# Three x blocks' second forms made during gate/up and kept in DRAM, loads asked earlier, some splits and streamed loads moved

## The chip, the cores and the metric

One core of one Trainium2 chip runs the whole kernel in one launch. The metric is the device time in microseconds, the median of three runs. The engines are named as in the profile: PE is TensorE (matmuls), DVE is VectorE, ACT is ScalarE, POOL is GpSimd (here it only issues DMAs), SP is SyncE (it issues DMAs).

## What is computed

```python
# x: [1, 2048, 512]; g = sigmoid of one dot product per row
g = sigmoid((x * gate_w).sum(-1, keepdims=True))
a = x @ dft_hid_re.T ; b = x @ dft_hid_im.T           # 512 x 512 each
fnet = dft_seq_re @ a - dft_seq_im @ b                # 2048 x 2048 each
h = silu(x @ w1) * (x @ w3)                           # 512 -> 1376
mlp = h @ w2                                          # 1376 -> 512
out = g * fnet + (1 - g) * mlp
```

All in fp32. The kernel splits each fp32 operand into a high part (rounded to fp32r, the type that the matmul takes) and a low part (the rest), and multiplies high x high, high x low and low x high, so each product costs three matmuls.

## The kernel before

**Block products.** Each product of 2 x 2 blocks takes seven block products in place of eight (a Strassen-like scheme with the sums T1 to T4 on one side and similar sums on the other). An operand therefore exists in forms: raw blocks and sums or differences of them, each split into a high part (`high`: a copy on ACT into fp32r) and a low part (`low`: a subtraction on DVE). A product of one 128-row weight half against a 512-wide operand is three matmuls (`mm3`, line 122), and a gate/up product is two such halves: six matmuls.

**Gate/up.** The hidden size is cut into 11 chunks and x into two halves g; `ITEMS` lists 22 pairs (chunk, half): chunks 0 to 8 with half 0, chunks 9 and 10 with both, then chunks 0 to 8 with half 1. Item 0 is written out by hand; `gate_up(n)` does items 1 to 21. Each full item issues seven products on PE: X += (wb form 4), Z = (wb form 5), `first1(n+3)`, X += (wb form 3), Z += (wa form 2), `first2(n+3)`, X += (wb form 6). The last three items have five. The bank X of item n is n modulo 4. Between the products, in program order, stand the reads of the banks: ACT copies X to u2 and Z to u4, DVE adds X to u4 and Z to u2, ACT applies Silu to X (line 399) and to the next gate (`gate1`, line 309), and POOL stores h to DRAM. TensorE adds onto Z again only after ACT has copied it.

The weights of an item come in two tiles. `wb` (4 forms) is made from the raw chunk with `sums_wb`, `high_wb`, `low_wb` and stored to `wbsp`; when chunks 1 to 8 come back for half 1 it is loaded from there (`load_wb`). `wa` (3 forms) is always split anew from the raw chunk `ws`, four items ahead; `back(w)` says that a set is one that comes back with its wb in DRAM. The split of wa stands between the product Z += and first2 (high, line 393) and behind first2 (low, line 397).

Further work is hung into the items by lists: `early` (behind the first product), `ahead`, `second`, `mid` (behind the fourth), `at_end`. In items 9 to 20 that is:

- `W2_AT` = items 9, 11, 13, 15: one pair of w2 row blocks. `load_w2` in at_end of the item before, `sums_w2` in early, `high_w2` in mid, and `low_w2` in early of the next item, which stores its two form tiles to `w2sp` (lines 568 and 571) and then frees them.
- `A1_AT` = items 12, 14, 16 to 20: the first forms of x block p. `load_a` in at_end of the item before, sums in early, `high_a` in mid, `low_a` in early of the next item.

Buffers are handed out in program order from two lists: `F4` (raw 4 KB tiles, `wide`) has four places in this stage, one of them held by a score row between items 8 and 13, and `ZO` (tiles of high and low parts, `parts`) has two, `zo_0` and `zo_1`. `take` hands out the place at the head of the list, and `free` puts it at the end, both while the program is written; on the chip the new user waits by semaphore until the old users, DMAs included, are done. DMA issues on one queue go out in program order, and one that waits holds those behind it.

**The streamed stage.** From 208 us on, eight streamed blocks follow: four of the sequence DFT (kind F), two of h (H), two of the hidden DFT (Y). Block 0 has seven products P1, P5, P6, P3, P7, P2, P4 of four steps each; a step is 12 matmuls against one raw tile of `cc` or one of its sums, split into a `zo` tile three steps ahead (`advance`: `load_c` eight steps ahead, `sum_c` four, `split_c` three). The static side is x: first forms A1 (made in gate/up) for P1, P5, P6, P3, and second forms A2 for P7, P2, P4. All eight A2 blocks are made in block 0 itself: `load_a2(p)` at step 4 + p, `sum2` at step 7 + p, `make_a2` (`forms2`, two high and two low operations) at step 8 + p. The first five cc tiles are asked with `load_c(0)` to `load_c(4)` at the ends of items 17 to 21.

Of the kernel before, what the change touches and what calls it, by code (L numbers as in the profile page):

```python
# [7 lines left out]
F32 = mybir.dt.float32  # L8
F32R = mybir.dt.float32r
# [3 lines left out]
P = 128  # L13
# [8 lines left out]
NG = NST // 2  # L22
# [4 lines left out]
K = 9  # L27
W2_AT = (9, 11, 13, 15)
A1_AT = (12, 14, 16, 17, 18, 19, 20)


@with_exitstack
def fnet_swiglu_gate_kernel(
# [20 lines left out]
    nc = tc.nc  # L54
# [11 lines left out]
    dram = ctx.enter_context(tc.tile_pool(name="dram", bufs=1, space=bass.MemoryType.DRAM))  # L66
# [13 lines left out]
    def bank(k, name):  # L80
        return psum.tile([P, 512], F32, tag=f"ps{k}", name=name)
# [8 lines left out]
    def take(places, shape, dtype, name):  # L90
        p, tag = at = places.pop(0)
        t = p.tile(shape, dtype, tag=tag, name=name)
        HELD[id(t)] = t, places, at
        return t
# [4 lines left out]
    def parts(name):  # L99
        return take(ZO, [P, 2, 4, 256], F32R, name)  # L100

    def free(*tiles):
        for t in tiles:
            _, places, at = HELD.pop(id(t))
            places.append(at)

    def high(hi, src):
        nc.scalar.activation(hi, src, AF.Copy)  # L108

    def low(hi, lo, src):  # L110
        nc.vector.tensor_sub(lo, src, hi.bitcast(F32))  # L111

    def split(hi, lo, src):
        high(hi, src)
        low(hi, lo, src)
# [16 lines left out]
    gs = dram.tile([NTB, 1, 512], F32, tag="gs", name="gs")  # L132
    gsp, ngsp = (dram.tile([2, P, 1024], F32, tag=k, name=k) for k in ("gsp", "ngsp"))
    dsp = [dram.tile([KD, P, 2, n, 256], F32, tag=f"dsp{n}", name=f"dsp{n}") for n in (4, 3)]
    w2sp = [dram.tile([NP2, P, 2, n, 256], F32, tag=f"w2sp{n}", name=f"w2sp{n}") for n in (4, 3)]
    wbsp = dram.tile([NC, P, 2, 4, 256], F32, tag="wbsp", name="wbsp")
    zsp = dram.tile([4 * NTB * P, 1024], F32, tag="zsp", name="zsp")
# [3 lines left out]
    def flat(ap):  # L141
        return ap.rearrange("p a n -> p (a n)")
# [29 lines left out]
    def sum2(r):  # L172

        nc.vector.tensor_sub(r[:, :256], r[:, 256:512], r[:, :256])

    def forms2(r, t2):

        r = r.rearrange("p (a n) -> p a n", a=4)
        split(flat(t2[:, 0, 0:2]), flat(t2[:, 1, 0:2]), flat(r[:, 2:4]))
        split(t2[:, 0, 2], t2[:, 1, 2], r[:, 0])  # L180
# [8 lines left out]
    NI = len(ITEMS)  # L189
# [35 lines left out]
    def back(w):  # L225
        return w >= NC and SETS[w] > 0

    def load_w(w, lo=0, hi=4):
        if lo == 0:
            WS[w] = f4_a.tile([P, 4, 256], F32, tag=f"f4_{4 + w % (LOOK + 1)}", name=f"ws{w}")  # L230
        nc.sync.dma_start(WS[w][:, lo:hi].rearrange("p a n -> p (a n)"),
                          w13[SETS[w], :, lo * 256 : hi * 256])

    def load_wb(w, spare=False):

        WB[w] = (parts(f"wb{w}") if spare else
                 wbp.tile([P, 2, 4, 256], F32R, tag="wb", name=f"wb{w}"))
        nc.sync.dma_start(WB[w].bitcast(F32), wbsp[SETS[w]])
# [31 lines left out]
    def prod(ps, n, wi, xi, start, chain=False):  # L270
        w = WSET[n]
        w, wi = (WA[w], wi) if wi < 3 else (WB[w], wi - 3)
        x = XO[ITEMS[n][1]]
        for q in range(2):
            sl = slice(q * P, (q + 1) * P)
            mm3(ps, w[:, 0, wi, sl], w[:, 1, wi, sl], x[:, 0, xi, q, :], x[:, 1, xi, q, :],
                start and q == 0, q == 1, chain)
# [3 lines left out]
    def first1(n):  # L281
        copy_x(n, prod1(n))
# [46 lines left out]
    def store_h(n, k, h):  # L329

        c, g = ITEMS[n]
        j = min(c % (NP2 - 1) if c < NC - 1 else NP2 - 1, NP2 - 1)
        b = 2 * (NP2 - 1 <= c < NC - 1)
        nc.gpsimd.dma_start(hsp[g, b + k, j // 2, :, j % 2 * 512 : (j % 2 + 1) * 512], h)  # L334
# [4 lines left out]
    early, ahead, second, mid, at_end = {}, {}, {}, {}, {}  # L339

    def run(work, n):
        for f in work.get(n, ()):
            f()

    def gate_up(n):
        last = NI - 1
        x, s1 = G.pop(n)
        z = bank(6 + n % 2, f"Z{n}")
        if n == last - 1:

            u2, g1 = (s1p.tile([P, 512], F32, tag="s1", name=f"{k}_{n}") for k in ("u2", "g1"))
        else:
            h = hp.tile([P, 1024], F32, tag="h", name=f"h{n}")
            u2, g1 = h[:, :512], h[:, 512:]
        u4 = u4p.tile([P, 512], F32, tag="u4", name=f"u4_{n}")
        nw = WSET[n + 1] if n < last else 0
        if nw in WB or nw == 0:
            nw = None
        elif back(nw):
            load_wb(nw)  # L360
            nw = None
        wa = WSET[n + LOOK + 1] if n + LOOK < last else 0
        if wa in WA or wa == 0:
            wa = None
        else:
            load_w(wa, 0, 3 if back(wa) else 4)

        prod(x, n, 4, 4, False, True)
        nc.scalar.activation(u2, x, AF.Copy)
        run(early, n)  # L370
        prod(z, n, 5, 5, True, True)
        run(ahead, n)
        nc.scalar.activation(u4, z, AF.Copy)
        run(second, n)
        if nw is not None:
            sums_wb(nw)
        if n + LOOK <= last:
            first1(n + LOOK)
        if nw is not None:
            high_wb(nw)  # L380
        prod(x, n, 3, 3, False, True)
        nc.vector.tensor_add(u4, u4, x)
        if nw is not None:
            low_wb(nw)
        run(mid, n)
        prod(z, n, 2, 6, False, True)
        nc.vector.tensor_add(u2, u2, z)
        nc.vector.tensor_mul(u2, s1, u2)  # L388
        store_h(n, 0, u2)
        if wa is not None:  # L390
            new_wa(wa)
            parts_a = wa_parts(wa, 0, 3)
            high(parts_a[0], parts_a[2])
        if n + LOOK <= last:
            first2(n + LOOK)
        if wa is not None:
            low(*parts_a)
        prod(x, n, 6, 2, False, True)
        nc.scalar.activation(g1, x, AF.Silu)
        put_score(n, 1, x)  # L400
        if n + LOOK <= last:
            gate1(n + LOOK)
        nc.vector.tensor_mul(g1, g1, u4)
        store_h(n, 1, g1)
        run(at_end, n)


# [109 lines left out]
    def do(work, n, f, *a):  # L517
        work.setdefault(n, []).append(lambda: f(*a))
# [55 lines left out]
    A1, A2, XR = [], [], {}  # L574
# [13 lines left out]
    def low_a(p):  # L588
        low(*parts_a1(p))
        free(XR.pop(p))  # L590

    for n in range(NI):
        if n in W2_AT:
            p = W2_AT.index(n)
            do(at_end, n - 1, load_w2, p)
            do(early, n, sums_w2, p)
            do(mid, n, high_w2, p)
            do(early, n + 1, low_w2, p)
        if n in A1_AT:
            p = A1_AT.index(n)  # L600
            do(at_end, n - 1, load_a, p)
            do(early, n, lambda p=p: sums1_here(XR[p]))
            do(mid, n, high_a, p)
            do(early, n + 1, low_a, p)
# [5 lines left out]
    n = NI - 1 - LOOK  # L610
    do(at_end, n - 1, F4.extend, [(f4_a, f"f4_{k}") for k in range(4, 5 + LOOK)])
    for k in range(LOOK + 2):
        do(at_end, n - 1 + k, lambda k=k: load_c(k))
    do(at_end, NI - 2, load_a, NG - 1)
    do(early, NI - 1, lambda: sums1_here(XR[NG - 1]))
    do(mid, NI - 1, lambda: split_c(0))
# [86 lines left out]
    def load_c(m):  # L703
        while LOADS and LOADS[0][0] <= m and F4:
            _, blk, k, q = LOADS.pop(0)
            r = RAW[blk, k, q] = wide(f"{k}_{blk}_{q}")
            n = cols(blk, q, k)
            nc.sync.dma_start(r[:, :n], block(blk, k, q)[:, :n])
# [15 lines left out]
    a2_cm, a2 = pool("a2", 1, "right")  # L724
    ut_cm, ut = pool("ut", 1, "right")
    F4[:0] = [(f4_b, f"f4_{k}") for k in range(5 + LOOK, 13)]
    ZO[:0] = [(zo_b, f"zo_{k}") for k in range(2, 4)]
    def load_a2(p):


        if p < NG // 2:
            t = a2.tile([P, 2, 3, 256], F32, tag=f"a2_{p + NG // 2}", name=f"xs{p}")
            XR[p] = t.rearrange("p h a n -> p (h a n)")[:, :1024]
        elif p < NG - 2:
            XR[p] = flat(ut.tile([P, 2, 512], F32, tag=("u3", "c21")[p % 2], name=f"xs{p}"))
        else:
            XR[p] = wide(f"xs{p}")
        nc.sync.dma_start(XR[p], xn[p])

    def make_a2(p):  # L740
        A2.append(a2.tile([P, 2, 3, 256], F32R, tag=f"a2_{p}", name=f"a2_{p}"))
        r = XR.pop(p)
        forms2(r, A2[p])
        if p >= NG - 2:
            free(r)

# [199 lines left out]
    def at(blk, n, f, *a):  # L946
        todo.setdefault(START[blk] + n, []).append((f, a))

    at(1, 1, load_score, 1)
    for p in range(NG):  # L950
        at(0, 4 + p, load_a2, p)

        at(0, 7 + p, lambda p=p: sum2(XR[p]))
    for p in range(NG):
        at(0, 8 + p, make_a2, p)

    at(0, 0, lambda: nc.scalar.activation(act0, act0, AF.Sigmoid))
# [3 lines left out]
    for i, (src, sp, p) in enumerate(late):  # L961
        blk, b = 1 + i // 2, i % 2
        n = (17, 24)[b]
# [11 lines left out]
    for p in range(KD):  # L975
        early = p < NG - NP2
# [76 lines left out]
```

## Time and profile before

| what | us |
|---|---|
| median of 3 runs (679.77 to 680.11) | 680.06 |
| the profiled execution | 679.73 |
| its span, first to last instruction | 678.0 |
| PE busy (3089 matmuls) | 671.2 |
| DVE busy | 602.1 |
| ACT busy | 366.9 |
| POOL busy | 64.0 |
| DMA moved | 172.54 MB, mean 255 GB/s |

How to read the lines that follow: a timeline line has the start in us, the length in us, the engine, the line of the kernel, the operation, output<-input by the program's names, shapes, how many were merged, and in brackets the engine's idle time before it and what ended it. A line of a waits view names who waited for whom, with the total, the number of times and the longest. A windows line has the stretch, its length, busy time and number of instructions of PE, PEld, DVE, ACT and POOL, then the granted clock of TensorE, the DMA share and GB/s. A line of a DMA view ends with the KB of one transfer and the us from its issue to its landing.

### The profile page before, as it was taken

What the parts mean: (1) busy time and instruction counts of PE and PEld (TensorE: products, weight loads), DVE (VectorE), ACT (ScalarE), POOL (GpSimd) and SP (SyncE); (2) the same over time, 40 slices, a digit from 0 to 9 for tenths busy, and PEclk for the clock granted to TensorE, in tenths of its full rate; (3) what the DMA queues carried; (4) which work ended last, traced back from release to release, by engine and by line L of the source; (5) the groups of instructions that cost most, each with busy time, mean ns of one, the idle gap of its engine ahead of it and who ended that gap; (6) DMA issues with size and microseconds to landing.
All of it is one profiled execution on the core that took longest, in us unless ns stands there. A gap on an engine that the chain in (4) does not pass through costs nothing.

```text
span 678.0 us, 8627 instructions
## 1 busy us (share of the span) xinstructions
PE 671.2 (99%) x3089; PEld 581.8 (86%) x3089; DVE 602.1 (89%) x737; ACT 366.9 (54%) x480; POOL 64.0 (9%) x118
## 2 busy tenths in 40 slices
PE   9999999999999999999999999999999999999997
PEld 6888888888888888888888888888888888888886
DVE  6999988787679999987999799979998897898996
ACT  6675566655446764464554554554546455445452
POOL 0011112121110000000110001100110000000000
PEclk9999999999999999999999999999999999999999
DMA  7585557499998656912497328915999982874942
GB/s 294 205 306 218 218 196 277 187 328 388 410 418 289 254 177 230 352 63 93 156 378 288 94 88 334 385 56 208 360 420 419 414 281 91 310 281 154 330 135 93
DMA packets 45547, 172.54 MB, mean 255 GB/s; under 512 B 5312, under 2 KB 5696, under 8 KB 41664
## 3 DMA queue, kind: packets, MB, share of 16 engines
q1 hardware_dynamic: 32608, 118.63, 48.2%
q0 software_dynamic: 12608, 52.97, 19.6%
q8 instruction: 24, 0.39, 0.2%
q10 hardware_dynamic: 288, 0.39, 0.2%
q14 instruction: 19, 0.16, 0.1%
HBM read 114.82 MB, written 57.16 MB: 254 GB/s over the span
## 4 chain that ended last, share of the span: by engine, by line
PE 51%; issue 37%; DMA 6%; DVE 3%; POOL 3%; ACT 0%; SPq 0%; POOLq 0%; DVEq 0%; ACTq 0%
PE P L122 24%; PE X L122 15%; PE Z L122 8%; PE Y L122 3%; DMA B<-hsp 2%; DMA dsp<-late_0l 2%; DMA xs_B<-xt 1%; POOL zsp L821 1%; DMA p5g<-gs 1%; POOL dsp L803 1%; POOL w2sp L803 1%; DVE wa L111 1%; DVE xs_B L214 1%; DVE zo L111 0%; DVE xo L111 0%
## 5 line engine op out<-in xcount | busy, mean ns | idle before, releaser
L122 PE MATMUL P<-zo,a 128*128 128x512 f32 x1344 | 290.9, 379 | 1.0 <-DVE zo L111 1.0
L122 PEld LDWEIGHTS P<-zo,a 128*128 128x128 f32 x1344 | 253.7, 189 | 38.0 <-DVE zo L111 2.0
L108 ACT ACTIVATE zo<-B 128x1024 fp32r<-128x1024 f32 (+1 forms) x182 | 188.4, 1041 | 180.2 <-DVE B L682 83.5
L111 DVE TENSOR_TENSOR zo<-B,zo 128x1024 fp32r<-128x1024 f32 (+1 forms) x182 | 217.2, 1201 | 30.9 <-ACT zo L108 30.2
L122 PE MATMUL P<-zo,H 128*128 128x512 f32 x468 | 101.4, 379 | 0.1
L122 PEld LDWEIGHTS P<-zo,H 128*128 128x128 f32 x468 | 88.4, 189 | 13.0 <-DVE zo L111 0.5
L682 DVE TENSOR_TENSOR B<-B,B 128x1024 f32<-128x1024 f32 (+1 forms) x78 | 92.7, 1188 | 1.2 <-DMA B<-hsp 1.1
L122 PE MATMUL X<-xo,wb 128*128 128x512 f32 x378 | 89.2, 380 | 0.2 <-DVE xo L111 0.2
L122 PEld LDWEIGHTS X<-xo,wb 128*128 128x128 f32 x378 | 71.1, 189 | 11.3 <-DVE xo L111 0.6
L122 PE MATMUL P<-zo,Y 128*128 128x512 f32 x336 | 72.7, 379 | 0.0
L122 PEld LDWEIGHTS P<-zo,Y 128*128 128x128 f32 x336 | 63.5, 189 | 9.0
L334 POOL DMA_DIRECT2D hsp<-h x42 | 23.0, 548 | 121.0 <-DVE h L388 67.7
L685 DVE TENSOR_TENSOR B<-B,B 128x1024 f32<-128x1024 f32 x26 | 31.6, 1217 | 0.0
L122 PE MATMUL X<-xo,wa 128*128 128x512 f32 x126 | 31.0, 381 | 0.1
L122 PE MATMUL Y<-xo,wa 128*128 128x512 f32 x126 | 30.6, 379 | 0.0
L122 PE MATMUL Z<-xo,wb 128*128 128x512 f32 x126 | 30.6, 379 | 0.0
L122 PE MATMUL Z<-xo,wa 128*128 128x512 f32 x126 | 30.6, 379 | 0.0
L913 ACT ACTIVATE zu<-P 128x512 f32<-128x512 f32 x32 | 19.0, 595 | 17.3 <-PE P L122 15.7
L111 DVE TENSOR_TENSOR wa<-ws,wa 128x768 fp32r<-128x768 f32 (+1 forms) x22 | 19.3, 880 | 9.6 <-ACT wa L108 9.5
L122 PEld LDWEIGHTS X<-xo,wa 128*128 128x128 f32 x126 | 23.5, 189 | 4.4 <-DVE wa L111 0.5
L122 PEld LDWEIGHTS Y<-xo,wa 128*128 128x128 f32 x126 | 23.8, 189 | 3.4
L122 PEld LDWEIGHTS Z<-xo,wb 128*128 128x128 f32 x126 | 23.8, 189 | 3.4
(137 smaller groups left out, 544.3 us busy)
## 6 DMA issues: line engine op xcount, KB each, us to landing
B<-cc SPq DMA_DIRECT2D x64, 512.0 KB, 6.4
hsp<-h POOLq DMA_DIRECT2D x42, 256.0 KB, 3.8
B<-hsp SPq DMA_DIRECT2D x20, 512.0 KB, 10.9
wbsp<-wb POOLq DMA_DIRECT2D x8, 1024.0 KB, 4.3
wb<-wbsp SPq DMA_DIRECT2D x8, 1024.0 KB, 8.3
B<-zsp SPq DMA_DIRECT2D x16, 512.0 KB, 8.2
H<-w2sp SPq DMA_DIRECT2D x6, 1024.0 KB, 9.4
ws<-w SPq DMA_DIRECT2D x11, 512.0 KB, 4.8
```

The lines of the kernel that those rows point to most:

```text
L108: nc.scalar.activation(hi, src, AF.Copy)
L111: nc.vector.tensor_sub(lo, src, hi.bitcast(F32))
L122: nc.tensor.matmul(ps.rearrange("p (n a) -> p n a", a=2), u, turns(v), **kw)
L214: nc.vector.tensor_sub(t, *(ST[g, v] for v in SUMS[k]))
L334: nc.gpsimd.dma_start(hsp[g, b + k, j // 2, :, j % 2 * 512 : (j % 2 + 1) * 512], h)
L682: nc.vector.tensor_add(t, t, RAW[blk, b, q][:, :n])
L685: nc.vector.tensor_sub(t, RAW[blk, "B12", q], t)
L803: nc.gpsimd.dma_start(flat(dst[:, k]), v[:, : 1024 - 256 * j].bitcast(F32))
L821: return nc.gpsimd.dma_start(z_rows(blk, k), flat(t))
L913: nc.scalar.activation(U[name][:, r], ps[r], AF.Copy)
```

## The change

Three of the eight x blocks (p = 0, 1, 2) get their second forms during gate/up, in items 12, 14 and 10. `sums_a2` takes a place from `ZO`, computes the one difference into its spare fourth, splits both parts and stores three forms to a new DRAM tile `a2sp`, all in `early` of the item, behind the `low_w2` that stands there already; `end_a2` frees the place in the next item. In block 0 these three blocks are loaded ready-made, and their `sum2` and `make_a2` are gone. `load_a` is asked two items ahead where no second form is made in the item; the x block of item 10 is loaded once more for its first forms in item 16. For sets that come back (`back`), the split of wa moves from around first2 to the end of the item, behind the store of h. The first five `load_c` move one item later, with the last two both at the end of item 21.

```diff
+A2_AT = (12, 14, 10)
...
+    a2sp = dram.tile([len(A2_AT), P, 2, 3, 256], F32, tag="a2sp", name="a2sp")
...
         if wa is not None:
             new_wa(wa)
             parts_a = wa_parts(wa, 0, 3)
-            high(parts_a[0], parts_a[2])
+            if not back(wa):
+                high(parts_a[0], parts_a[2])
         if n + LOOK <= last:
             first2(n + LOOK)
-        if wa is not None:
+        if wa is not None and not back(wa):
             low(*parts_a)
...
         store_h(n, 1, g1)
+        if wa is not None and back(wa):
+            split(*parts_a)
         run(at_end, n)
...
+    A2E = {}
+
+    def sums_a2(p):
+        t = A2E[p] = parts(f"a2e{p}")
+        r, d = XR[p], t[:, 0, 3].bitcast(F32)
+        nc.vector.tensor_sub(d, r[:, 256:512], r[:, :256])
+        for i, j, v in ((0, 2, r[:, 512:]), (2, 3, d)):
+            split(flat(t[:, 0, i:j]), flat(t[:, 1, i:j]), v)
+        nc.gpsimd.dma_start(a2sp[p], t[:, :, :3].bitcast(F32))
+
+    def end_a2(p, alone):
+        free(A2E.pop(p))
+        if alone:
+            free(XR.pop(p))
...
+        if n in A2_AT:
+            p = A2_AT.index(n)
+            if n not in A1_AT:
+                do(at_end, n - 1, load_a, p)
+                do(early, n, sums_a2, p)
+                do(early, n + 1, end_a2, p, True)
         if n in A1_AT:
             p = A1_AT.index(n)
-            do(at_end, n - 1, load_a, p)
+            do(at_end, n - (1 if n in A2_AT else 2), load_a, p)
+            if n in A2_AT:
+                do(early, n, sums_a2, p)
+                do(early, n + 1, end_a2, p, False)
...
     for k in range(LOOK + 2):
-        do(at_end, n - 1 + k, lambda k=k: load_c(k))
+        do(at_end, min(n + k, NI - 1), lambda k=k: load_c(k))
...
     def load_a2(p):
+        if p < len(A2_AT):
+            nc.sync.dma_start(new_a2(p).bitcast(F32), a2sp[p])
+            return
...
-        at(0, 7 + p, lambda p=p: sum2(XR[p]))
-    for p in range(NG):
+        if p >= len(A2_AT):
+            at(0, 7 + p, lambda p=p: sum2(XR[p]))
+    for p in range(len(A2_AT), NG):
         at(0, 8 + p, make_a2, p)
```

`new_a2(p)` makes the A2 tile and appends it to the list; `make_a2` now calls it too.

More of the change, by code (lines that the diff above doesn't have):

```diff
@@ L727, in fnet_swiglu_gate_kernel, with new_a2 @@
     ZO[:0] = [(zo_b, f"zo_{k}") for k in range(2, 4)]
+    def new_a2(p):
+        A2.append(a2.tile([P, 2, 3, 256], F32R, tag=f"a2_{p}", name=f"a2_{p}"))
+        return A2[p]
     def load_a2(p):
+        if p < len(A2_AT):
+            nc.sync.dma_start(new_a2(p).bitcast(F32), a2sp[p])
+            return
         if p < NG // 2:
@@ L740, in make_a2 @@
     def make_a2(p):
-        A2.append(a2.tile([P, 2, 3, 256], F32R, tag=f"a2_{p}", name=f"a2_{p}"))
         r = XR.pop(p)
-        forms2(r, A2[p])
+        forms2(r, new_a2(p))
         if p >= NG - 2:
```

## The prediction

> **What bounds the kernel now.** First the head of the page, then TensorE's timeline around its holes.
>
> ```profile
> span 678.0 us, 8627 instructions
> ...
> PE 671.2 (99%) x3089; PEld 581.8 (86%) x3089; DVE 602.1 (89%) x737; ACT 366.9 (54%) x480; POOL 64.0 (9%) x118
> ```
>
> TensorE is busy for 99% of the span. The change neither adds nor removes a matmul, so it can only fill holes between matmuls or open new ones. A product of six matmuls starts 1.29 us after the last one (111.77 to 113.06 in a fence below), or 0.2158 us each; against that pace, starts that lie further apart are holes. The timeline of PE shows two places that the change touches, late in gate/up and late in the first streamed block:
>
> ```profile
> 177.81 2.93 PE L122 MATMUL X<-xo,wb 128*128 128x512 f32 x12
> 180.57 1.46 PE L122 MATMUL Z<-xo,wb 128*128 128x512 f32 x6
> 182.17 1.64 PE L122 MATMUL X<-xo,wa 128*128 128x512 f32 x6
> 183.65 1.46 PE L122 MATMUL X<-xo,wb 128*128 128x512 f32 x6
> ...
> 247.76 4.97 PE L122 MATMUL P<-zo,a 128*128 128x512 f32 x22
> 253.42 2.86 PE L122 MATMUL P<-zo,a 128*128 128x512 f32 x12 [0.69 <-DVE zo L111]
> 256.63 1.56 PE L122 MATMUL P<-zo,a 128*128 128x512 f32 x6 [0.35 <-DVE zo L111]
> ```
>
> At pace 12, 6 and 6 matmuls take 2.59, 1.29 and 1.29 us; the starts lie 2.76, 1.60 and 1.48 apart, so 0.66 us is lost near 182. At 253 and 257 it is 5.66 - 22 x 0.2158 = 0.91 and 3.21 - 12 x 0.2158 = 0.62, or 1.5 us, and VectorE's low part of a streamed block is named as the releaser. All that the change can win is about 2.2 us. The windows view and VectorE's groups of this block (208 to 257 us) tell why:
>
> ```profile
> 249.90:259.00 9.10, 8.06 (x36) 6.45 (x36) 9.03 (x12) 4.80 (x6) 0.00 (x0) 1.00 0.80 260
> ...
> L111 DVE TENSOR_TENSOR a<-xs,a 128x512 fp32r<-128x512 f32 (+1 forms) x16 | 8.2, 552 | 0.0
> L174 DVE TENSOR_TENSOR xs<-xs 128x256 f32<-128x256 f32 x8 | 3.3, 418 | 0.0
> ```
>
> VectorE (third busy figure) has 9.03 us of work in 9.10 us; the second forms of the eight x blocks take 8.2 + 3.3 = 11.5 us, 1.44 us a block.
>
> **Part 1, the work taken out of the first block.** Three blocks fewer: 3 x 1.44 = 4.3 us of VectorE, ahead of the late low parts. These are late by at most 0.91 + 0.62 us in all, so both holes close: -1.5 us. Next in line is VectorE itself, with some 2.8 us in hand. The three finished forms come back by three loads of 768 KB in place of 512 KB; they land where the earliest product that reads them is still P7, 16 steps into the block.
>
> **Part 2, where the work goes.** sums_a2 stands in the list "early" of items 10, 12 and 14, right behind low_w2, which stores a pair of second-half weights. In gate/up only two places for parts exist (zo_0 and zo_1). low_w2 frees both, and sums_a2 takes the front one, which is always that of w2a. So its first instructions on VectorE and on ScalarE may not write before the 1 MB store of w2a has been read out and has landed. Item 10 before:
>
> ```profile
> 108.10 0.58 ACT L369 ACTIVATE h<-X 128x512 f32<-128x512 f32 x1
> ...
> 108.52 0.95 DVE L111 TENSOR_TENSOR w2a<-w2m,w2a 128x768 fp32r<-128x768 f32 x1
> ...
> 109.38 0.60 ACT L373 ACTIVATE u<-Z 128x512 f32<-128x512 f32 x1 [0.70 <-PE Z L122]
> 109.39 1.02 DVE L111 TENSOR_TENSOR w2b<-w2r,w2b 128x512 fp32r<-128x512 f32 x2
> ...
> 110.10 0.55 POOL L568 DMA_DIRECT2D w2sp<-w2a  x1 [0.89 <-ACT u L373]
> ...
> 111.77 1.46 PE L122 MATMUL Z<-xo,wa 128*128 128x512 f32 x6
> ...
> 113.06 1.46 PE L122 MATMUL Y<-xo,wa 128*128 128x512 f32 x6
> ```
>
> The store leaves at 110.10; VectorE reaches the new instruction at about 110.4. ScalarE reaches its high part at 108.7, ahead of the copy of Z (109.38), which stands behind it in ScalarE's order. TensorE adds onto that Z at 111.77 and cannot go on before the copy. How long such a store takes (column last: KB, us to landing; the first three are the w2a stores of items 10, 12 and 14, the fourth the tile's min/median/max, the fifth the nearest store of that size from the page):
>
> ```profile
> w2sp<-w2a POOLq DMA_DIRECT2D x1, 1024.0 KB, 5.7
> ...
> w2sp<-w2a POOLq DMA_DIRECT2D x1, 1024.0 KB, 6.2
> ...
> w2sp<-w2a POOLq DMA_DIRECT2D x1, 1024.0 KB, 7.8
> ...
> DMA to landing us min/median/max: 5.7/6.9/7.8
> ...
> wbsp<-wb POOLq DMA_DIRECT2D x8, 1024.0 KB, 4.3
> ```
>
> That this is a true wait, the trace shows once, where the same places meet a later store:
>
> ```profile
> 158.42 0.94 ACT L108 ACTIVATE w2b<-w2r 128x512 fp32r<-128x512 f32 x2 [0.72 <-DMA w2sp<-w2b]
> ```
>
> After the landing ScalarE has a 512-wide and a 256-wide high part (0.62 and 0.40; the row just above has the two as 0.94) and the copy of Z (0.60): Z is free 1.55 us after the landing.
>
> Item 10: in the changed kernel w2r and a w13 load run beside this store, as w2r did in item 12, so I take 6.2: 110.10 + 6.2 + 1.55 = 117.85, against 111.77: **6.1 us late**.
>
> **Part 3, the wa parts moved to the item's end.** Before, and at the change from item 10 to 11:
>
> ```profile
> 112.86 0.83 ACT L108 ACTIVATE wa<-ws 128x768 fp32r<-128x768 f32 x1
> ...
> 115.85 0.60 ACT L399 ACTIVATE h<-X 128x512 f32<-128x512 f32 x1 [2.16 <-PE X L122]
> ...
> 116.06 0.95 DVE L111 TENSOR_TENSOR wa<-ws,wa 128x768 fp32r<-128x768 f32 x1
> 116.34 0.62 ACT L309 ACTIVATE s<-s 128x512 f32<-128x512 f32 x1
> ...
> 116.95 1.46 PE L122 MATMUL Z<-xo,wb 128*128 128x512 f32 x6
> ...
> 118.24 0.59 PE L122 MATMUL X<-xo,wa 128*128 128x512 f32 x2
> ...
> 106.28 0.64 ACT L323 ACTIVATE sc<-s 32x512 f32<-32x512 f32 x1 [1.36 <-DVE s L305]
> ```
>
> Item 11 starts at 116.95 - 1.29 = 115.66. After: Silu ends 116.45, the next gate's Silu 116.96, then high (0.83) 117.75 and low (0.95) 118.7. The first product with these parts starts at 118.24 and uses the low part in its third matmul, 0.43 later, at 118.67. So the move has no slack left: 0.1 to 0.2 us of new wait in each of the items 11, 14, 15, 16 and 17 (0.8 in all). Where the score row is copied first (0.64, ends of items 11 and 12) it is 0.7, and 1.05 behind item 12, where VectorE is still catching up (an estimate: half an operation of 0.69 more). The gain of the move is near 182, where the Silu that frees the bank stood behind high, and high behind a late load:
>
> ```profile
> 180.79 0.84 ACT L108 ACTIVATE wa<-ws 128x768 fp32r<-128x768 f32 x1 [5.07 <-PE X L122]
> 181.54 0.58 ACT L399 ACTIVATE h<-X 128x512 f32<-128x512 f32 x1
> ```
>
> The Silu no longer waits, so the 0.66 goes; next is that load: high still starts near 180.8, low ends near 182.6, and the matmul due at 182.1 waits 0.45. Sum of the waits: 0.8 + 0.7 + 1.05 + 0.45 = 3.0, less 0.66.
>
> The move also delays items 12 and 14, since low_w2 stands behind the wa low:
>
> ```profile
> 126.49 0.95 DVE L111 TENSOR_TENSOR w2a<-w2m,w2a 128x768 fp32r<-128x768 f32 x1
> ...
> 129.90 1.46 PE L122 MATMUL Z<-xo,wa 128*128 128x512 f32 x6
> ```
>
> Item 12 starts four products before 129.90, at 124.72 = S. The low part at 126.49 came 1.58 us ahead of its store, as in item 10, so the store left at S + 3.35. With the chain of Silu, score row, Silu, high and low, low_w2 starts about 2.1 us later: the store leaves at S + 5.45, lands at 6.2 more, Z is free at S + 13.2; due it was at S + 5.18 + 0.7: **7.3 us late**. Item 14 has no score row (4.8), more transfers beside it (the median 6.9 taken between its own 7.8 and the others): S + 13.25 against S + 5.4, **7.9 us late**. Behind each wait VectorE's queue (sums, u4 + X, the wb low part) ends just within the products that follow.
>
> **Part 4, the clock.** Windows view at the end (clock is the third figure from the right), and the first matmuls:
>
> ```profile
> 676.00:677.00 1.00, 0.00 (x0) 0.00 (x0) 0.00 (x0) 0.00 (x0) 0.00 (x0) 0.69 0.44 146
> ...
> 0.78 4.10 PE L414 MATMUL wps<-const-bfloat16-1.0 128*128 128x512 bf16 x11 [0.78 <-PEq L1042]
> ```
>
> The last product ends at about 674.1, and a mean of 0.69 in 676 to 677 is half clock from 676.4 on, 2.3 us later. The eleven matmuls from rest took 4.10 us, against about 2.5 at pace: 1.6 us lost. All three waits are far longer than 2.3 us: 3 x 1.6 = 4.8. The trace of before has no such wait in mid-kernel, so the bounds are 0 and twice this. [...]
>
> **Part 5, the queues.** On SP the x loads move ahead of the wb and ws loads of the next item. Those wb loads wait for TensorE anyway, so they lose nothing; the x loads wait for places that low_w2 or low_a frees, before that. The first cc loads are asked one item later, but all except the last two still ahead of the last item. On POOL the three a2sp stores stand ahead of h stores that are not yet due. The x block of item 10 is read once more (512 KB). I cost all this at nothing, and a win is excluded, as no load of this stretch but the ws of Part 3 ends a hole. The cover is the slack between load and use; gone, it would cost a load's 5 to 10 us once.
>
> **The sum.** 6.1 + 7.3 + 7.9 + 3.0 - 0.66 + 4.8 - 1.5 = +26.9 us. The profiled execution took 679.73, the median is 680.06: 706.6 for an execution like the profiled one, **707.0** against the median.
>
> **The rivals.** (a) Shorter stores: at 4.3 us each the three waits lose 1.9 + 1.9 + 2.6 = 6.4, and with a clock that stays full another 4.8: 695.8, the low end. Either half alone gives 701 to 702. For: that row is of the same size. Against: it ran without loads beside it. (b) Longer: stores of 7.8 (+1.6 +1.6 +0.9 = 4.1) and a clock at half for twice the time (+4.8): 716. For it speaks that the DMA share rises with the added 768 KB stores. (c) Faster: the wait never binds, because the place is really free when sums_a2 comes. Then 680.06 - 1.5 - 0.66 = 677.9, and Part 3's waits, which lie within 0.2 us of none in most items, on top: 678 to 680.6, at the likeliest 678.6. It decides itself at Z: the store would have to land by 111.77 - 1.55 = 110.2, 0.1 us after it leaves, or another place be taken. (d) The change does not do what it says: the holes at 253 and 257 stay since something else (the cc loads asked later) is late; +1.5 on the forecast, within its range.
>
> **How the numbers follow.** Forecast (703 to 711) 0.5; (a) 0.27; (b) with (d) 0.18; (c) 0.04; 0.01 for no change. Measurements of this kernel can tell about 0.2%. The range runs from 697 to 716: it leaves out (c), the far end of (a) and what lies beyond (b). Faster 0.04, same 0.01, slower 0.95.
>
> **What would show it.** In TensorE's timeline three holes of 6 to 8 us in items 10, 12 and 14, each ahead of a product that adds to Z; in the waits ScalarE or VectorE on a2e released by DMA w2sp<-w2a; a granted clock under 1 behind each; the holes near 253 and 257 gone. I am wrong if a2e starts without waiting for that store, or if TensorE passes it.

## The result, and the profile after

The changed kernel takes 710.38 us (median; 709.37 to 711.18) against 679.91 for the kernel before: ratio 1.0451, 95% interval 1.0438 to 1.0464. The profiled execution took 710.54 us, its span 708.8. The prediction was 707.0, between 697 and 716.

The head of the page, with the granted clock in the 40 slices:

```profile
span 708.8 us, 8636 instructions
...
PE 680.7 (96%) x3089; PEld 586.5 (83%) x3089; DVE 603.8 (85%) x737; ACT 366.7 (52%) x480; POOL 66.0 (9%) x121
...
PEclk9999998988899999999999999999999999999999
```

TensorE has the same 3089 matmuls, is idle for 21 us more, and its clock is below 90% of full in four slices (17.7 us each), from the seventh to the eleventh. The waits views name who is waited for, in TensorE's rows and in ScalarE's (95 to 245 us):

```profile
PE Z L123 <- ACT u L375: 20.8, 3, 8.8
...
ACT a2e L109 <- DMA w2sp<-w2a: 17.7, 2, 10.3
ACT a2e L109 <- issue: 7.7, 1, 7.7
```

TensorE waits three times for the copy of Z, ScalarE three times ahead of the high part of a2e, and for two of these the profile names the store of w2a. The third, in item 10, has no releaser in the view, but its timeline shows the same chain:

```profile
109.95 0.55 POOL L573 DMA_DIRECT2D w2sp<-w2a  x1 [0.89 <-DVE w2a L112]
...
116.27 0.63 ACT L109 ACTIVATE a2e<-xr 128x512 fp32r<-128x512 f32 x1 [7.74 <-issue]
116.28 0.42 DVE L603 TENSOR_TENSOR a2e<-xr 128x256 f32<-128x256 f32 x1 [6.02 <-issue]
116.81 0.40 ACT L109 ACTIVATE a2e<-a2e 128x256 fp32r<-128x256 f32 x1
...
117.11 0.58 ACT L375 ACTIVATE u<-Z 128x512 f32<-128x512 f32 x1
...
117.74 1.22 PE L123 MATMUL Z<-xo,wa 128*128 128x512 f32 x2 [5.96 <-ACT u L375]
```

The store that leaves at 109.95 is the one of 6.2 us in the first row below, so it lands at 116.2; both engines start on a2e 0.07 us later, and Z is free at 117.7. The three stores, in items 10, 12 and 14:

```profile
w2sp<-w2a POOLq DMA_DIRECT2D x1, 1024.0 KB, 6.2
...
w2sp<-w2a POOLq DMA_DIRECT2D x1, 1024.0 KB, 5.3
...
w2sp<-w2a POOLq DMA_DIRECT2D x1, 1024.0 KB, 7.8
```

The windows view of the holes (first, third, fifth line) and of the stretch behind each (clock third from the right):

```profile
111.60:117.70 6.10, 0.19 (x1) 0.00 (x0) 1.19 (x3) 1.43 (x4) 0.04 (x1) 0.93 0.95 346
117.70:123.70 6.00, 5.96 (x14) 4.78 (x15) 5.23 (x10) 1.53 (x2) 0.88 (x2) 0.50 0.94 322
139.90:146.10 6.20, 0.27 (x2) 0.00 (x0) 1.14 (x3) 1.38 (x4) 0.68 (x1) 0.84 0.92 319
146.10:151.00 4.90, 4.81 (x11) 3.86 (x12) 4.27 (x10) 2.37 (x4) 0.68 (x1) 0.50 0.61 242
167.80:176.80 9.00, 0.24 (x2) 0.00 (x0) 1.17 (x3) 1.41 (x4) 0.82 (x2) 0.70 0.95 389
176.80:181.70 4.90, 4.83 (x11) 3.86 (x12) 3.44 (x7) 1.56 (x3) 0.74 (x2) 0.50 0.41 161
```

Behind each hole TensorE runs for 4.8 to 5.9 us at half clock (first stretch: 14 matmuls in 6.00 us, where 0.2158 each would be 3.0). In the first streamed block the two holes are gone; one merged line of the timeline holds 187 matmuls, at 0.2167 each:

```profile
249.77 40.52 PE L123 MATMUL P<-zo,a 128*128 128x512 f32 x187
```

From the starts of the matmuls, against a pace of 0.2158 us, by the prediction's own terms:

| term | forecast, us | measured, us |
|---|---|---|
| Z late in item 10 | 6.1 | 6.1 |
| Z late in item 12 | 7.3 | 6.2 |
| Z late in item 14 | 7.9 | 9.0 |
| first1 waiting for wa (items 11 to 18) | 3.0 | 2.9 |
| hole near 182 | -0.66 | -0.66 |
| slow matmuls behind the three holes | 4.8 | 7.9 |
| first streamed block | -1.5 | -1.6 |
| the hole near 508 of before | 0 | +0.5 |
| sum | 26.9 | 30.4 |

The last matmul starts 30.25 us later than before (673.67 to 703.92).

### The profile page after: what moved, and what is told of

It reads as the page before. It is cut to its first block, busy times and chain, and to the rows that moved or that the text cites. A ratio compares the mean times of both kernels' runs of the same rounds, so it can differ in the third digit from the quotient of the medians.

```text
span 708.8 us, 8636 instructions
## 1 busy us (share of the span) xinstructions
PE 680.7 (96%) x3089; PEld 586.5 (83%) x3089; DVE 603.8 (85%) x737; ACT 366.7 (52%) x480; POOL 66.0 (9%) x121
## 4 chain that ended last, share of the span: by engine, by line
PE 68%; DMA 5%; DVE 2%; issue 1%; ACT 1%; POOL 0%; ACTq 0%; DVEq 0%; POOLq 0%
PE P L123 60%; PE X L123 5%; PE Z L123 3%; DMA B<-hsp 2%; DMA dsp<-late_0l 2%; DMA w2sp<-w2a 1%; PE Y L123 1%; DVE zo L112 1%; DVE zc L855 0%; DVE B L712 0%; ACT zo L109 0%; ACT a2e L109 0%; DVE c21p L154 0%; DVE w2a L112 0%; ACT late_0h L109 0%
## 5 line engine op out<-in xcount | busy, mean ns | idle before, releaser
L123 PE MATMUL Z<-xo,wa 128*128 128x512 f32 x126 | 35.0, 419 | 20.8 <-ACT u L375 20.8
L123 PEld LDWEIGHTS Z<-xo,wa 128*128 128x128 f32 x126 | 25.9, 209 | 26.0 <-ACT u L375 22.0
L123 PE MATMUL Y<-xo,wa 128*128 128x512 f32 x126 | 34.0, 410 | 0.0
L123 PE MATMUL X<-xo,wa 128*128 128x512 f32 x126 | 32.6, 388 | 0.8 <-DVE wa L112 0.6
L123 PEld LDWEIGHTS Y<-xo,wa 128*128 128x128 f32 x126 | 26.5, 210 | 4.5
L402 ACT ACTIVATE h<-X 128x512 f32<-128x512 f32 x20 | 11.9, 597 | 33.3 <-PE X L123 33.3
L949 ACT ACTIVATE zu<-P 128x512 f32<-128x512 f32 x32 | 19.1, 596 | 18.2 <-PE P L123 16.2
```

What stands on the lines that cost most here:

```text
L123: nc.tensor.matmul(ps.rearrange("p (n a) -> p n a", a=2), u, turns(v), **kw)
L949: nc.scalar.activation(U[name][:, r], ps[r], AF.Copy)
```

## The experiments

The theory: sums_a2 takes the ZO place that low_w2 has just given up, its first operations wait for the 1 MB store out of that place, the copy of Z waits behind them on ScalarE, and TensorE behind that. The rivals: the added work itself is what costs, or the moved split, or the moved loads. The kernel before took 679.60 to 679.71 us (medians) beside these runs.

**Two of the three in places of their own.**

```diff
-        t = A2E[p] = parts(f"a2e{p}")
+        t = A2E[p] = (parts(f"a2e{p}") if p == 2 else
+                      a1.tile([P, 2, 4, 256], F32R, tag=f"a1_{6 - p}", name=f"a2e{p}"))
...
```

> The changed kernel, but sums_a2 of items 12 and 14 writes into a place of its own (an A1 tile that is not used before items 19 and 20); item 10 keeps the place freed by low_w2. Theory (the wait for the w2a store): the holes of 6.2 and 9.0 us in items 12 and 14 and the half clock behind each (2.45 and 2.5 us) go, that of item 10 stays. In their place stays the wait of ScalarE's second high part for VectorE's difference behind low_w2, some 1.3 us in each. 710.4 - 20.1 + 2.6 = 692.9, between 690 and 695. Rival (the added work on VectorE and ScalarE costs the time, wherever it is written): above 705, with the holes still there.

694.18 us, ratio 1.0214 (1.0199 to 1.0230). Two of the three holes close to 1.25 us each, the one of item 10 stays at 6.1, and the mean granted clock is 0.995, against 0.982 in the changed kernel. TensorE's waits:

```profile
PE Z L123 <- ACT u L375: 7.9, 3, 6.0
```

The work is the same and the place alone differs, so the place is what costs: the theory's number, not the rival's. In item 12 a2e now starts at 136.52 on ScalarE, while the store of w2a lands only at 144.30.

**The moved split alone**, on the kernel before:

```diff
-            high(parts_a[0], parts_a[2])
+            if not back(wa):
+                high(parts_a[0], parts_a[2])
...
+        if wa is not None and back(wa):
+            split(*parts_a)
```

> The kernel before with one part of the change: the split of wa moved to the end of the item for sets that come back. Theory: first1 of the next item waits 0.2 us in most items and some 0.9 where the score row is copied, 2.9 in all, less the 0.66 us hole near 182 that goes: 2.2 us slower than before, 682.2. Rival (the move is paid by the slack and only gains): 679.4.

683.82 us, ratio 1.0060 (1.0044 to 1.0077): slower than either expected. Item 12 shows why:

```profile
134.11 2.88 PE L122 MATMUL X<-xo,wb 128*128 128x512 f32 x12 [0.44 <-DVE u L382]
136.83 1.46 PE L122 MATMUL Z<-xo,wb 128*128 128x512 f32 x6
139.18 0.70 PE L122 MATMUL X<-xo,wa 128*128 128x512 f32 x2 [0.89 <-ACT wa L108]
```

and on ScalarE, ahead of that wa:

```profile
137.76 0.63 ACT L309 ACTIVATE s<-s 128x512 f32<-128x512 f32 x1 [0.84 <-DVE s L305]
138.30 0.83 ACT L108 ACTIVATE wa<-ws 128x768 fp32r<-128x768 f32 x1
```

Without long holes VectorE has no time to catch up; its sum of u4 and X comes 0.7 late in item 12. The high part of the wa that item 13 needs stands behind a Silu that waits for VectorE too, and TensorE loses 1.7 there (0.9 in the changed kernel). There these waits are smaller or absent, since TensorE stands or runs slowly just then.

**TensorE kept busy in the holes.**

```diff
+FILL = {10: 24, 12: 24, 14: 36}
...
         prod(x, n, 3, 3, False, True)
+        if n in FILL:
+            fill = bank(6 + (n + 1) % 2, f"fill{n}")
+            for _ in range(FILL[n]):
+                nc.tensor.matmul(fill, warm[:, :P], warm, start=True, stop=True)
```

> The changed kernel with idle matmuls on a bank nobody reads, behind the fourth product of items 10, 12 and 14 (24, 24 and 36 of them, 5.2, 5.2 and 7.8 us at pace), so that TensorE works through most of each hole. Theory (half clock after the holes costs 7.8 us, the holes themselves 21.3): the clock stays full, 710.4 - 7.8 = 702.6. Rival (the slow matmuls behind the holes come from late operands, not from the clock): 710 or more.

709.24 us (706.90 to 711.41), ratio 1.0435 (1.0409 to 1.0462): the expected 702.6 was missed. The clock did stay full in the profiled execution (mean 0.999), here behind the three holes:

```profile
117.60:123.60 6.00, 5.97 (x28) 5.25 (x29) 5.40 (x11) 2.12 (x3) 0.90 (x2) 1.00 0.90 321
144.50:149.50 5.00, 4.22 (x18) 3.42 (x19) 4.37 (x10) 2.47 (x3) 0.69 (x1) 1.00 0.57 229
175.50:180.50 5.00, 4.88 (x23) 4.29 (x24) 4.07 (x10) 2.31 (x5) 1.25 (x2) 1.00 0.40 157
```

28 matmuls pass in the 6.00 us that held 14. But more than half of the 7.9 us is lost again elsewhere. In the profiled executions, first1 of item 11 now waits 1.5 (0.2 before), the last product of item 12 waits 1.0 for VectorE, first1 of item 13 waits 1.7 (0.9), and the third hole is 0.9 longer with its store. So the last matmul is only 3.6 us earlier than in the changed kernel, and that in the fastest of the four executions (706.90), the one that was profiled. Half clock and VectorE's lag lie over each other; taking one away uncovers the other. The medians differ by 1.1 us, less than the runs scatter, so what the clock alone is worth in this kernel is not settled; no execution gained the expected 7.8.

**The moved loads alone.**

```diff
-            do(at_end, n - 1, load_a, p)
+            do(at_end, n - (1 if n in (12, 14) else 2), load_a, p)
...
-        do(at_end, n - 1 + k, lambda k=k: load_c(k))
+        do(at_end, min(n + k, NI - 1), lambda k=k: load_c(k))
```

> The kernel before with the moved loads alone: x blocks asked two items ahead (except in items 12 and 14) and the first five streamed loads one item later. Theory: no cost and no gain, 680.0 within 0.5. Rival (a late streamed block or wb load): 1 to 6 us slower, with a new hole near 208.

680.02 us, ratio 1.0006 (0.9997 to 1.0015): no cost that can be told apart. The hole of 0.66 at 182 is gone here too, without a moved split; one of 0.5 stands at 163, and that near 508 is 0.5 longer.

**All three in places of their own.**

```diff
-A2_AT = (12, 14, 10)
+A2_AT = (12, 14, 16)
...
-        t = A2E[p] = parts(f"a2e{p}")
+        t = A2E[p] = a1.tile([P, 2, 4, 256], F32R, tag=f"a1_{6 - p}", name=f"a2e{p}")
...
```

> The changed kernel with all three sums_a2 in places of their own (A1 tiles not used yet), in items 12, 14 and 16, still in the list early and with the split of wa still at the item's end. Theory: none of the three long holes and no half clock; what is left over the kernel before is the split (4.0 measured alone), ScalarE's wait of 1.25 in each of three items, less the 1.6 of the first block: 679.6 + 4.0 + 3.75 - 1.6 = 685.8. Rival (the added work itself): above 700.

686.51 us, ratio 1.0100 (1.0086 to 1.0113), as the theory has it. What is left at Z:

```profile
PE Z L123 <- ACT u L375: 3.0, 3, 1.0
```

**The change with the split put back.**

```diff
-            if not back(wa):
-                high(parts_a[0], parts_a[2])
+            high(parts_a[0], parts_a[2])
...
-        if wa is not None and back(wa):
-            split(*parts_a)
```

> The changed kernel with the split of wa back where it was. Theory: the three long holes stay (about 6.1, 6 and 8 us, since low_w2 and its store come up to 2 us earlier in items 12 and 14 while the due time comes 0.9 earlier), the waits of first1 (2.9 in all) go and the hole near 182 comes back: 710.4 - 2.9 + 0.7 - 1 = 707. Rival (the split at the end of the item is what delays Z): back to 682 or so.

706.40 us, ratio 1.0391 (1.0377 to 1.0405). The three waits for Z stay:

```profile
PE Z L123 <- ACT u L375: 20.4, 3, 9.2
```

Without the moved split the time is 4.0 us lower, and the long holes stay. In the traces the last matmul is 3.7 us earlier: 2.9 of it are the waits of first1, 0.4 the three holes together, 0.4 the hole near 508. One expectation failed: the hole near 182 did not come back, so the moved loads close it without the split.

The hole of item 10 is 6.1 us here as in the changed kernel, but the half clock behind it ends sooner, 3.8 us after TensorE starts again and not 5.9 (clock third from the right):

```profile
117.90:121.60 3.70, 3.70 (x9) 2.97 (x10) 3.14 (x7) 2.21 (x3) 0.68 (x1) 0.50 0.85 306
121.70:123.70 2.00, 2.00 (x10) 1.76 (x10) 1.97 (x4) 0.00 (x0) 0.06 (x1) 1.00 0.96 370
```

**Behind the copy of Z.** Two versions with the sums in the list second, in items 12, 14 and 16 and in places of their own: the first is the one above with the split moved for the last set alone, the second is built on the kernel before without any moved load or split. From the second:

```diff
+A2_AT = (12, 14, 16)
...
-            do(early, n, lambda p=p: sums1_here(XR[p]))
+            if n in A2_AT:
+                do(second, n, sums_a2, p)
+            do(second if n in A2_AT else early, n, lambda p=p: sums1_here(XR[p]))
```

> As all_own, but sums_a2 and the sums behind it stand in the list second (behind the copy of Z), and the split of wa is moved for the last set alone, where the Silu stood behind a late load. Theory: the copy of Z waits for nothing new, the holes at 253 and 257 go (1.6) and most of that at 182 (0.5): 677.5, with up to 1 us for VectorE's longer queue in item 12. Rival (VectorE has no room for 4.3 us in gate/up): 681 or more, with new holes in items 12 to 14.

> The kernel before with the second forms of three x blocks made in items 12, 14 and 16 in places of their own, in the list second; no moved split, no moved loads. Theory: -1.6 in the first block, the hole at 182 stays: 678.0, with up to 1 us for item 12. Rival (without the x blocks asked earlier the sums wait for their load): 680 or more, with ScalarE or VectorE waiting for xr.

683.24 (ratio 1.0051, 1.0038 to 1.0063) and 683.16 us (1.0048, 1.0034 to 1.0062): both missed, and the first one's rival (VectorE has no room) was right. The second one's was not: VectorE waits for an x block once, for 0.6. TensorE's waits in the second:

```profile
PE X L123 <- DVE u L384: 1.6, 3, 0.9
PE X L123 <- ACT h L401: 1.5, 2, 0.8
...
PE X L123 <- DMA wb<-wbsp: 0.7, 1, 0.7
```

The wait at Z is gone, but in items 12, 14 and 16 the last product waits for the sum of u4 and X, which now stands behind 2.6 us of sums on VectorE (1.3 before). The other two rows are a Silu behind a high part that waits for its raw load, and a wb load that lands late. The new 768 KB stores took 12.3 us to land at the median; that they are what delays those loads was not tried by itself.

**One block, where there is room.** One x block (p = 4), in item 18, which splits no wa, in the list mid, behind the sum of u4 and X; moved loads; then also the split moved for the sets 17 and 19 alone:

```diff
+A2_P, A2_N = 4, 18
...
+            if n == A2_N:
+                do(mid, n, sums_a2, p)
+            do(mid if n == A2_N else early, n, lambda p=p: sums1_here(XR[p]))
...
+LATE_W = (17, 19)
...
-            high(parts_a[0], parts_a[2])
+            if wa not in LATE_W:
+                high(parts_a[0], parts_a[2])
...
```

> The kernel with the moved loads alone (no cost measured), and the second form of one x block (p = 4) made in item 18, where no wa is split: in the list mid, behind the sum of u4 and X that TensorE waits for, in a place of its own. Theory: 1.44 us less of VectorE in the first streamed block closes the hole at 253 (0.9) and leaves about 0.2 of that at 257 (0.6); no new hole in gate/up: -1.3, 678.4. Rival (no item of gate/up has room, or the store makes a load late there): 680 or more, with a hole between 185 and 208.

> As one, and the split of wa moved to the item's end for two sets alone (17 and 19), where the Silu stood behind a split that waits for a late load. Theory: a hole of 0.5 becomes one of 0.2 in each place where one is: 0.3 to 0.6 below one, 678.0. Rival (a moved split delays VectorE's further work of the item): equal to one or above.

678.96 (ratio 0.9989, 0.9980 to 0.9998) and 678.76 us (0.9986, 0.9977 to 0.9995). The second is below both kernels of this study; its lead over the kernel before is 0.14%, with an interval that ends at 0.9995, too little to call it faster. In the first streamed block one hole of 0.36 us is left of 1.6, as the theory has it; 0.6 us is lost in gate/up all the same (a hole of 0.8 near 163). For the split of two more sets the rival was right: in the traces gate/up ends 0.3 later with it, and the last matmul is 0.35 earlier only because the hole near 508 is 0.6 shorter.

## Why the prediction was right

The path was the forecast one, step by step. **Part 1** held: the two holes closed (1.6 us for 1.5). **Part 2** held in its mechanism and nearly in its sum: 21.3 us of waiting for Z, forecast and measured. That agreement is better than its terms: item 12 was 1.1 too high, since its store landed in 5.3 us and not in 6.2, and item 14 was 1.1 too low, since I took 6.9 where its own row of before, 7.8, was right. Item 10 agrees to 0.1, the store taking the 6.2 us assumed. **Part 3** agrees in the changed kernel (2.9 for 3.0), but the agreement is partly luck: alone on the kernel before, the moved split cost 4.0 us in the traces (4.2 by the medians), because VectorE's lag in items 12 and 13, which the prediction put at 1.75 for both, is about 3.4 when TensorE gives it no time. The gain of 0.66 near 182 has the right size, but the moved split, which the prediction named as its cause, was not needed for it: the moved loads close that hole alone as well.

**Part 4** is the term that was mis-sized. I took 1.6 us a hole from the eleven first matmuls; it was 2.5 to 3.0, in all 7.9 for 4.8. The half clock lasted 4.8 to 5.9 us behind each hole. The price is not one number that a single place can give: the hole of item 10, 6.1 us in the changed kernel and with the split put back, was followed by 5.9 us at half clock in the first and by 3.8 in the second (the last section shows when the clock changes). At the start of the kernel before, the first record of a full clock begins at 3.96 us, 3.2 us after the first matmul at 0.78: sooner than behind each of the changed kernel's holes. That the clock halves in mid-kernel, the changed kernel shows three times, in holes of 6.1, 6.2 and 9.0 us; the trace of before showed a fall only behind its last matmul. The filled holes show in turn that this term cannot simply be added: less than half of it was won by them (3.6 us of 7.9 in the profiled executions).

**Part 5** held, the moved loads cost nothing that can be told apart, with one late surprise: the hole near 508 grew by 0.5 us. It did so with the moved loads alone, but not with the same loads in the last kernel above, so its cause stays open. The order of the issues on SP, on which this part counts, shows in the kernel before: the w2r load of 128.44 waits 16.2 us for w2b, and no DMA leaves SP between 111.89 and that time.

Of the rivals, (c) is refuted: the store landed 6 us too late for it, and with the wait removed the change was still no gain. (d) is refuted too, since both holes of the first block closed. (a) and (b) bound the stores as they came, 5.3 to 7.8 us. The row of 4.3 us that (a) rests on is a median of eight stores of the kernel before: seven took 4.2 to 4.6 us beside h stores and the ends of loads, and the one that ran beside parts of four loads took 7.1.

## What to carry to other kernels

A place that was freed in the program is not free on the chip while a store still reads it, so before new work is hung into a list, look up which place it will get, who used that place last, and what stands behind the new work on its engine: here waits of 7 to 10 us on ScalarE became waits of 6 to 9 us on TensorE, because one small copy stood behind the new work. Where the first engine is busy 99% of the time, set what a change can win at most (2.2 us here) against the slack of the stage that receives the work; one block moved to an item with room cost nothing (678.8 us), three moved to items that were full cost 3.5 us (683.2).

## What the runs showed of the hardware that was not expected

After a hole TensorE stayed at half clock for 4.8 to 5.9 us in the changed kernel, longer than the 3.2 us from the first matmul to the first record of a full clock in the kernel before. The clock fell 5.1, 4.0 and 3.4 us after the last matmul's end in the holes of items 10, 12 and 14 (means 0.93, 0.84 and 0.70 in the windows), and behind the last matmul 3.0 us after its end there, against 2.3 us at the end of the kernel before. With filler matmuls in the holes the clock was 1.00 behind all three in the profiled execution; of the other three executions two have a mean of 0.997, one of 1.000.

The times at which the granted clock changes show a pattern in the two traces of the kernel before and the changed kernel. In the changed kernel it changes at 116.85, 123.67, 144.15, 150.98, 171.46 and 181.70 us: the distances of 6.83, 20.48, 6.83, 20.48 and 10.24 are 2, 6, 2, 6 and 3 times 3.413 (20.48 / 6). The fall behind its last matmul, at 707.35, comes 154 such steps after 181.70, and in the kernel before the one fall, at 676.39, comes 197 after the first record of a full clock at 3.96. Behind the three holes TensorE starts again at 117.74, 146.19 and 176.87 us and the clock is full at 123.67, 150.98 and 181.70: each time at the second of these steps after the start. With the split put back TensorE starts at 117.88, and the windows above have the clock full from 121.70 on. So in these two runs what a hole cost differed with when it ended: TensorE ran at half clock for 3.8 to 5.9 us and lost half of that. What sets the times of the steps, no run shows. From the first matmul to the first record of a full clock it took 3.2 us in the kernel before, which is behind the prediction's 1.6, and 3.4 in the changed kernel.
